# A speech codec kernel on one core: the silu's add of one on the pool engine, more updates on the vector engine, transposes and accumulating transfers taking turns

## The chip, the core and the metric

The kernel runs on one core of a Trainium2 chip. The metric is the device time of one execution in microseconds. The engines are named as the profile names them: PE is the tensor engine, DVE the vector engine, ACT the scalar engine, POOL the pool engine (GpSimd) and SP the engine that here only issues transfers. Each engine runs its own instructions in the order in which they were emitted.

## The reference

The input x is 2 x 16000 x 512 in bf16. The kernel must compute a depthwise convolution of three taps along time, a silu, four stages of residual vector quantization with eight code words each, and a second depthwise convolution of three taps over the sum of the chosen words:

```python
B, T, D, K = 2, 16000, 512, 3
Nq, C = 4, 8
z = sum(xp[:, i:i+T, :] * dw_enc[i] for i in range(K))
z = silu(z)
res, q = z, 0
for s in range(Nq):
    cb = codebooks[s]
    d2 = |res|^2 - 2 * res @ cb.T + |cb|^2
    sel = cb[d2.argmin(-1)]
    q, res = q + sel, res - sel
y = sum(qp[:, i:i+T, :] * dw_dec[i] for i in range(K))
```

## The kernel before

The 32000 tokens are cut into 250 groups of 128 tokens, and the groups into 16 chunks: one of 12 groups, 14 of 16, and one of 14 that is worked on as 16. The 512 channels are four channel blocks of 128. The encoder works with the channels on the partitions, so a tile of one channel block of a full chunk is 128 x 2048 bf16.

For each chunk:

- `load` brings x in transposed, by DMA transposes of four groups each that SP issues (line 486), into the tile XT. Chunk 0 is loaded as rows and turned on PE instead.
- `front` does the first convolution and the silu, one channel block at a time in `block(i)`. DVE multiplies by each of the three taps (line 553) into the tiles Z and T. The two sums Z + T are made either on DVE (line 561) or by an accumulating DMA that POOL issues (line 559); from chunk 1 on, the first sum of all four blocks and the second sum of block 3 are named in `DMA_ADDS`, five accumulating transfers a chunk. The silu is z / (1 + exp(-z)): ACT takes exp(-z) (line 565), an add of one follows on DVE (line 569), ACT takes the logarithm (line 573) and exp of its negative (line 576), and DVE multiplies with z into RES (line 581).
- `stage` runs four times. PE scores the tokens against the code words (lines 637 and 643), DVE reduces and picks the nearest word (lines 651 to 697), PE turns the one-hot choice (line 707) and DVE copies it (line 714). Then the residual is updated for each of four channel blocks, in two halves: either PE makes the chosen words alone and DVE adds them to RES (line 747, one operand from SBUF and one from PSUM), or PE adds RES and the words itself and ACT copies the result back (line 758). How many of the four blocks go by DVE in each of the first three stages is written in `ON_DVE`, and in `ON_DVE_LAST` for the last three chunks; the chunk's number picks the entry. The fourth stage has no update.
- `finish` makes the output by products of the one-hot choices with prepared tables (line 785), ACT copies them out of PSUM (line 791), and SP issues the stores (line 795).

The order of the work on each engine isn't written by hand. Every piece is a task of the class `Plan`, with an engine, a cost, a latency, what it needs, a due time and the buffers that it takes and gives. `Plan.run` simulates the tasks forwards and backwards from a seeded random start (`ROUNDS`) and emits the instructions in the order that comes out. All transfers are tasks of one server, "DMA". When the kind changes between transposes (RUNS, kind 1) and accumulating transfers (ADDS, kind 2), the plan adds a gap of up to `APART`, and it weighs such a gap by `CLUMP` when it picks the next transfer. What the hardware itself must wait for is set in `keep_apart`: each transpose waits for an accumulating transfer issued before it, and the other way round, and `LAG` says which one, counted back from the last.

Buffers: four of Z, five of T, three of E, one of LN, two of XT, three of YSB.

Of the kernel before, what the change touches and what calls it, by code (L numbers as in the profile page):

```python
# [13 lines left out]
ALU = mybir.AluOpType  # L14
# [11 lines left out]
SIZES = [12] + [16] * 14 + [14]  # L26


ON_DVE = [(1, 2, 2)]
ON_DVE_LAST = [(2, 2, 2)]  # L30
LAST = 3

# [3 lines left out]

EARLY = 1

RUN = 4

AHEAD = 40
# [2 lines left out]
PERIOD, LEAD, STAGE, LATE, SPREAD = 56, 0.4, 0.9, 0.3, 0.3  # L44
FAR = -3.3e38

ROUNDS = [(940, 0.3, 0.0, 7), (4101, 0.3, 2.0, 9), (5991, 0.3, 0.0, 7), (15520, 0.3, 0.0, 10)]


CELLS, COLUMNS, ROWS = range(3)  # L50
WHOLE = (CELLS, CELLS, 0, 0.0)
SWITCH, CLING, SLOW = 0.1, 10.0, 1.08
RUNS, ADDS = (1, 1, 0, 0.0), (2, 2, 0, 0.0)
APART, CLUMP = 0.5, 2.0

LAG = 2


class Plan:
# [18 lines left out]
    def pass_over(self, rank, backward=False):  # L78

        tasks = self.tasks  # L80
        needs = [t[3] for t in tasks]
        after = [[] for _ in tasks]
        for n, ds in enumerate(needs):
            for d in ds:
                after[d].append(n)
        if backward:
            needs, after = after, needs
        takes, gives = (7, 6) if backward else (6, 7)
        left = [len(d) for d in needs]
        engines = list(dict.fromkeys(t[0] for t in tasks))  # L90
        ready = {e: [] for e in engines}
        until = {e: 0.0 for e in engines}
        slots = dict(self.slots)
        for n, t in enumerate(tasks):
            if not left[n]:
                heapq.heappush(ready[t[0]], (rank[n], n))
        now, events, order, starts, before = 0.0, [], [], [0.0] * len(tasks), WHOLE
        sort, ended = 0, 0.0
        while True:
            going = True  # L100
            while going:
                going = False
                for e in engines:
                    if until[e] > now + 1e-9:
                        continue
                    passed, pick, least, gap = [], None, 0.0, 0.0
                    while e == "DMA" and ready[e]:
                        at, n = heapq.heappop(ready[e])
                        passed.append((at, n))
                        if all(slots[k] > 0 for k in tasks[n][takes]):  # L110
                            kind, lost = tasks[n][8][0], 0.0
                            if kind and sort and kind != sort:
                                lost = max(0.0, APART - (now - ended))
                            if pick is None or at + CLUMP * lost < least:
                                pick, least, gap = n, at + CLUMP * lost, lost
                    while e == "PE" and ready[e]:
                        at, n = heapq.heappop(ready[e])
                        passed.append((at, n))
                        if all(slots[k] > 0 for k in tasks[n][takes]):
                            here = tasks[n][8]  # L120
                            lost = self.between(here, before) if backward else self.between(before, here)
                            if pick is None or at + CLING * lost < least:
                                pick, least, gap = n, at + CLING * lost, lost
                    if pick is not None:
                        passed = [v for v in passed if v[1] != pick]
                        if e == "PE":
                            before = tasks[pick][8]
                        elif tasks[pick][8][0]:
                            sort, ended = tasks[pick][8][0], now + gap + tasks[pick][1]
                    while pick is None and ready[e]:  # L130
                        at, n = heapq.heappop(ready[e])
                        if all(slots[k] > 0 for k in tasks[n][takes]):
                            pick = n
                            break
                        passed.append((at, n))
                    for p in passed:
                        heapq.heappush(ready[e], p)
                    if pick is None:
                        continue
                    t = tasks[pick]  # L140
                    for k in t[takes]:
                        slots[k] -= 1
                    order.append(pick)
                    starts[pick] = now
                    until[e] = now + gap + t[1]
                    heapq.heappush(events, (now + gap + t[1], -1))
                    heapq.heappush(events, (now + gap + max(t[1], t[2]), pick))
                    going = True
            if len(order) == len(tasks):
                return starts, order  # L150
            now = events[0][0]
            while events and events[0][0] <= now + 1e-9:
                _, n = heapq.heappop(events)
                if n < 0:
                    continue
                for k in tasks[n][gives]:
                    slots[k] += 1
                for a in after[n]:
                    left[a] -= 1
                    if not left[a]:  # L160
                        heapq.heappush(ready[tasks[a][0]], (rank[a], a))
# [46 lines left out]
def kernel(  # L208
# [8 lines left out]
    nc = tc.nc  # L217
# [255 lines left out]
    def load(st, org):  # L473
        plan.part += 1
        g0, G, GP = st["g0"], st["G"], st["GP"]
        done = []
        if g0 == 0:
            load_rows(st, org)
            return

        def place():
            st["XT"] = xpool.tile([P, GC + 2, KT, P], BF16, name="XT")

        def run(n, m):
            g = g0 + n - 1
            t = nc.sync.dma_start_transpose(out=st["XT"][:, n:n + m, :, :].rearrange("p n i t -> p (n i) t"),
                                        in_=xv[:, g:g + m, :].rearrange("p g d -> p (g d)"))
            keep_apart(t, runs, adds)

        def edge(n):  # L490
            st["XE"] = const.tile([P, KT, P], BF16, name="XE")
            keep_apart(nc.sync.dma_start_transpose(out=st["XE"], in_=group_rows(0)), runs, adds)

        def shift(n):
            XT, XE = st["XT"], st["XE"]
            nc.gpsimd.tensor_copy(XT[:, n, :, 0:P - 1], XE[:, :, 1:P])
            for b in range(B):
                p = (b + 1) * HB - 1
                nc.gpsimd.memset(XT[:, n, :, p:p + 1], 0.0)
            if GP > G:  # L500
                nc.gpsimd.memset(XT[:, G + 2:GP + 2, :, :], 0.0)

        def behind():
            nc.gpsimd.tensor_copy(st["XT"][0:1, 0, 0, 0:2], XR[0:1, 1, 0:2])
            nc.gpsimd.tensor_copy(st["XT"][0:1, 0, 0, 2:4], CB4[0:1, 0:2])
            for b in range(B):
                p = b * HB + 32
                nc.gpsimd.tensor_copy(st["XT"][p:p + 1, 0, 0, 0:2], XR[p:p + 1, 0, 0:2])

        room = plan.add("SP", 0.0, 0.0, [], org - 2.2 * PERIOD, place, take=("XT",))  # L510
        if st["n"] == 1:
            room = plan.add("POOL", 0.8, 1.0, [room, book, chunks[0]["rows"]], early, behind)
            gate.append(room)
        inside = min(G + 2, S + 1 - g0)
        for n in range(0, G + 2, RUN):
            due = org - 2.2 * PERIOD + 0.01 * n
            m = min(RUN, inside - n)
            if m > 0:
                done.append(plan.add("DMA", 0.7 * m, 2.7 + 0.7 * m, [room], due, lambda n=n, m=m: run(n, m), mode=RUNS))
        if inside < G + 2:  # L520
            t = plan.add("DMA", 0.9, 3.2, [room], due, lambda: edge(G + 1), mode=RUNS)
            st["edge"] = plan.add("POOL", 1.0, 1.4, [t], due, lambda: shift(G + 1))
        st["loaded"] = done + [st.get("edge")]

    def front(st, org):
# [3 lines left out]
        def dve(full):  # L529
            return 0.1 + (full - 0.1) * f  # L530
# [14 lines left out]
        def block(i):  # L545
            plan.part += 1
            u = {}

            def product(k):
                name = "ZTU"[k]  # L550
# [15 lines left out]

            def one():
                e = u["E"][:, 0:G, :]
                nc.vector.tensor_scalar(out=e, in0=e, scalar1=1.0, scalar2=None, op0=ALU.add)  # L569

            def log():
                u["LN"] = lnpool.tile([P, GC, P], F32, name="LN")
# [25 lines left out]
            st["taps"].append(t)  # L598
            z = add_up(2, [z, t])
            e = plan.add("ACT", act(1.8), act(1.8) + 0.12, [z], due, exp, take=("E",))  # L600
            e = plan.add("DVE", dve(0.6), dve(0.6) + 0.1, [e], due, one)
            e = plan.add("ACT", act(1.8), act(1.8) + 0.12, [e], due, log, take=("LN",))
            e = plan.add("ACT", act(1.8), act(1.8) + 0.12, [e], due, inverse, give=("LN",))
            r = plan.add("DVE", dve(1.13), dve(1.13) + 0.1, [e] + [t for t in st["silu"][-1:]], due, silu,
# [285 lines left out]
```

## Time and profile before

| | before |
|---|---|
| median of the runs shown (3) | 744.69 us |
| lowest, highest | 741.8, 744.74 us |
| the profiled execution's own time | 742.04 us |
| its span | 740.3 us |
| mean granted clock of PE | 0.934 |

A profile is taken of one execution. Its span reaches from the first to the last instruction, and the execution's own time, measured as the others, lies 1.7 us above it. A line of the groups names the line of code, the engine, the operation, output and inputs with their shapes, and the count; then the busy time in us and the mean duration of one in ns; then how long the engine had been idle just before such instructions, and what ended that. A line of the stretches gives the busy time of every engine between two times. A line of the order of time begins with start and duration in us.

### The profile page before, as it was taken

The numbers are of one execution on the slowest core, as the hardware profiler recorded it, in microseconds if no ns is written. First come the engines' busy times: TensorE is split into PE (matmuls) and PEld (weight loads), VectorE is DVE, ScalarE is ACT, GpSimd is POOL, SyncE is SP. The second block draws the span as 40 slices with busy tenths as digits, with TensorE's granted clock in tenths as the row PEclk, the third lists the DMA queues.
The fourth block names the chain that finished last, engine by engine and source line by source line (L and its number), as shares of the span: only waits on it lengthen the run. The fifth ranks groups of instructions, "written<-read, shape, count | busy, mean of one in ns | idle before, by whom it ended". The sixth has DMA issues, their size and how long they took to land. (4 is left out here: it accounts for less than half of the span.)

```text
span 740.3 us, 23586 instructions
## 1 busy us (share of the span) xinstructions
PE 590.8 (80%) x10478; PEld 314.2 (42%) x10544; DVE 685.9 (93%) x1359; ACT 665.4 (90%) x539; POOL 81.7 (11%) x104
## 2 busy tenths in 40 slices
PE   5037687787987888986978888878988898989996
PEld 5023334344444444434444444444453444444543
DVE  6999989899999999997999999989999999998952
ACT  2688979899999999998899999989999999976576
POOL 3112101111101011100101111100111101100000
PEclk9566969999999999999799899999999999999999
DMA  7969795859696967839978875959896435320234
GB/s 178 189 130 182 135 200 104 141 122 201 182 174 158 209 133 164 165 116 143 188 171 177 175 165 143 182 132 174 172 210 136 131 64 152 87 88 2 88 143 199
DMA packets 160833, 111.14 MB, mean 150 GB/s; under 512 B 142426, under 2 KB 142811, under 8 KB 160603
## 3 DMA queue, kind: packets, MB, share of 16 engines
q1 hardware_dynamic: 148976, 69.61, 39.5%
q0 software_dynamic: 11472, 39.76, 29.9%
q8 instruction: 82, 1.34, 0.8%
q10 hardware_dynamic: 282, 0.26, 0.1%
q14 instruction: 21, 0.16, 0.1%
HBM read 2.39 MB, written 32.77 MB: 47 GB/s over the span
## 5 line engine op out<-in xcount | busy, mean ns | idle before, releaser
L758 ACT ACTIVATE RES<-NEW 128x1024 bf16<-128x1024 f32 (+1 forms) x218 | 218.5, 1043 | 28.6 <-PE NEW L731 21.9
L747 DVE TENSOR_TENSOR RES<-RES,SEL 128x1024 bf16<-128x1024 bf16 (+1 forms) x166 | 197.5, 1203 | 6.7 <-PE SEL L731 6.3
L643 PE MATMUL PS<-RES 128*64 128x80 bf16 (+1 forms) x8064 | 176.1, 203 | 11.2 <-DVE RES L581 9.7
L643 PEld LDWEIGHTS <-RES 128*64 128x64 bf16 x8064 | 172.8, 115 | 19.6 <-DVE RES L581 10.6
L752 PE MATMUL NEW<-RES,IDENT 128*128 128x512 bf16 (+1 forms) x436 | 137.7, 399 | 31.3 <-ACT RES L758 15.6
L791 ACT ACTIVATE YSB<-Y 128x1024 bf16<-128x1024 f32 (+1 forms) x126 | 126.6, 1061 | 8.4 <-PE Y L785 4.5
L565 ACT ACTIVATE E<-Z 128x2048 bf16<-128x2048 bf16 (+1 forms) x64 | 123.2, 1931 | 11.5 <-DMA Z<-T 4.0
L559 POOL DMA_DIRECT2D Z<-T x75 | 72.9, 976 | 537.5 <-ACT RES L758 78.8
L573 ACT ACTIVATE LN<-E 128x2048 f32<-128x2048 bf16 (+1 forms) x64 | 123.0, 1923 | 9.9 <-DVE E L569 9.2
L576 ACT ACTIVATE E<-LN 128x2048 bf16<-128x2048 f32 (+1 forms) x64 | 123.0, 1922 | 0.4
L651 DVE TENSOR_REDUCE TR<-PS 128x5 bf16<-128x320 f32 (+1 forms) x188 | 96.0, 515 | 14.4 <-PE PS L643 14.3
L553 DVE TENSOR_SCALAR T<-XT,WENC 128x2048 bf16<-128x2048 bf16 (+1 forms) x128 | 94.8, 745 | 5.1 <-DMA Z<-T 5.1
L731 PEld LDWEIGHTS <-CBN 32*128 32x128 bf16 x768 | 32.6, 92 | 137.7 <-issue 134.3
L785 PE MATMUL Y<-A,OHT 128*128 128x512 bf16 x219 | 77.6, 382 | 16.4 <-ACT RES L758 6.0
L731 PE MATMUL NEW<-OHT,CBN 32*128 32x512 bf16 (+1 forms) x436 | 88.3, 402 | 0.1
L581 DVE TENSOR_TENSOR RES<-Z,E 128x2048 bf16<-128x2048 bf16 (+1 forms) x64 | 77.3, 1208 | 0.0
L731 PE MATMUL SEL<-OHT,CBN 32*128 32x512 bf16 (+1 forms) x332 | 58.7, 396 | 22.0 <-ACT RES L758 13.3
L637 PE MATMUL PS<-MASK,IDENT 128*64 128x320 bf16 (+1 forms) x376 | 64.6, 340 | 8.6 <-DVE PR L654 6.2
L561 DVE TENSOR_TENSOR Z<-Z,T 128x2048 bf16<-128x2048 bf16 (+1 forms) x53 | 62.5, 1181 | 2.7 <-DMA Z<-T 2.7
L752 PEld LDWEIGHTS <-IDENT 128*128 128x128 bf16 x436 | 33.1, 99 | 67.4 <-issue 57.4
L430 PE MATMUL PS<-MASK,IDENT 128*128 128x384 bf16 x167 | 46.2, 359 | 10.1 <-DVE PR L654 9.8
L785 PEld LDWEIGHTS <-OHT 128*128 128x128 bf16 x373 | 32.1, 97 | 50.8 <-issue 22.8
(78 smaller groups left out, 416.2 us busy)
## 6 DMA issues: line engine op xcount, KB each, us to landing
Z<-T POOLq DMA_DIRECT2D x75, 512.0 KB, 5.6
out_dram<-YSB SPq DMA_DIRECT2D x61, 512.0 KB, 3.2
RES<-in_x_dram SPq DMA_DIRECT2D x1, 1664.0 KB, 6.8
XT<-in_x_dram SPq DMA_TRANSPOSE x74, 5.7
out_dram<-YSB SPq DMA_DIRECT2D x1, 384.0 KB, 2.3
out_dram<-YSB SPq DMA_DIRECT2D x1, 256.0 KB, 2.7
A<-in_dw_dec_dram POOLq DMA_DIRECT2D x2, 96.0 KB, 6.4
CB<-in_codebooks_dram ACTq DMA_DIRECT2D x1, 128.0 KB
```

What stands on the lines that cost most here:

```text
L553: nc.vector.tensor_scalar(out=places(u[name]), in0=taps(i, k), scalar1=WENC[:, i, k:k + 1], scalar2=None, op0=ALU.mult)
L565: nc.scalar.activation(u["E"][:, 0:G, :], u["Z"][:, 0:G, :], ACT.Exp, scale=-1.0)
L573: nc.scalar.activation(u["LN"][:, 0:G, :], u["E"][:, 0:G, :], ACT.Ln)
L576: nc.scalar.activation(u["E"][:, 0:G, :], u["LN"][:, 0:G, :], ACT.Exp, scale=-1.0)
L643: nc.tensor.matmul(V[h * HT:(h + 1) * HT, r, :], lhsT=half[:, LC:LC + HT], rhs=half[:, lo:hi], start=False, stop=(i == KT - 1), skip_group ...
L651: nc.vector.tensor_reduce(out=u["TR"][:, q:q + m], in_=u["V", q][:, :, own:own + HT], axis=AX.X, op=ALU.max)
L731: nc.tensor.matmul(ps, lhsT=CBN[s][rows, i * P:(i + 1) * P], rhs=u["OHT"][rows, 0:MB, :], start=start, stop=True, skip_group_check=True)
L747: nc.vector.tensor_tensor(out=old, in0=old, in1=u["SEL", i, j][:, :, 0:W].rearrange("p h (m t) -> p h m t", t=HT), op=ALU.add)
L752: nc.tensor.matmul(NEW[:, h, 0:W], lhsT=IDENT, rhs=tokens(i, j + h, 1), start=True, stop=False, skip_group_check=True)
L758: nc.scalar.activation(old, u["NEW", i, j][:, :, 0:W].rearrange("p h (m t) -> p h m t", t=HT), ACT.Copy)
L785: nc.tensor.matmul(Y[:, h, :], lhsT=lhs(), rhs=rhs, start=(a == 0), stop=(a == len(terms) - 1))
L791: nc.scalar.activation(u["YSB"][:, k:k + n, :], u[k][:, 0:n, :], ACT.Copy)
```

## The change

Four things are changed, and the seeds of the plan with them.

- From chunk 1 on, the add of one is issued on POOL in all four channel blocks, and the plan counts 2.4 us for it; in chunk 0 it stays on DVE.
- `ON_DVE` gets a second entry. Chunks 0, 2, ..., 12 take (2, 2, 2), chunks 1, 3, ..., 11 take (1, 2, 2) as before. The last three chunks are unchanged.
- `LAG` goes from 2 to 1: a transpose now waits for the last accumulating transfer issued before it rather than the last but one, and an accumulating transfer for the last transpose.
- In the plan, the gap after a change of kind becomes 1.9 us towards transposes and 2.3 us towards accumulating transfers, where it was 0.5 us, and the cost of a transpose falls from 0.7 to 0.6 us a group.

```diff
-ON_DVE = [(1, 2, 2)]
+ON_DVE = [(2, 2, 2), (1, 2, 2)]
 ON_DVE_LAST = [(2, 2, 2)]
...
+ONE_ON_POOL = (0, 1, 2, 3)
+POOL_ONE = 2.4
...
-ROUNDS = [(940, 0.3, 0.0, 7), (4101, 0.3, 2.0, 9), (5991, 0.3, 0.0, 7), (15520, 0.3, 0.0, 10)]
+ROUNDS = [(520, 0.3, 3.0, 9), (1278, 0.3, 0.0, 8), (1401, 0.3, 2.0, 6)]
...
-APART, CLUMP = 0.5, 2.0
-
-LAG = 2
+APART = (0.0, 1.9, 2.3)
+CLUMP = 2.0
+
+LAG = 1
...
-                                lost = max(0.0, APART - (now - ended))
+                                lost = max(0.0, APART[sort if backward else kind] - (now - ended))
...
-                done.append(plan.add("DMA", 0.7 * m, 2.7 + 0.7 * m, [room], due, lambda n=n, m=m: run(n, m), mode=RUNS))
+                done.append(plan.add("DMA", 0.6 * m, 2.4 + 0.6 * m, [room], due, lambda n=n, m=m: run(n, m), mode=RUNS))
...
+            on_pool = st["n"] >= EARLY and i in ONE_ON_POOL
...
             def one():
                 e = u["E"][:, 0:G, :]
-                nc.vector.tensor_scalar(out=e, in0=e, scalar1=1.0, scalar2=None, op0=ALU.add)
+                where = nc.gpsimd if on_pool else nc.vector
+                where.tensor_scalar(out=e, in0=e, scalar1=1.0, scalar2=None, op0=ALU.add)
...
-            e = plan.add("DVE", dve(0.6), dve(0.6) + 0.1, [e], due, one)
+            if on_pool:
+                e = plan.add("POOL", dve(POOL_ONE), dve(POOL_ONE) + 0.3, [e], due, one)
+            else:
+                e = plan.add("DVE", dve(0.6), dve(0.6) + 0.1, [e], due, one)
```

## The prediction

> **What bounds the kernel now.** I read four views in this order: the page's busy times, the busy time by stretches, the groups of instructions with shapes kept apart, and the list of what the vector engine waited for. Then I went to the order of time around the one place where the pool engine already does arithmetic on a whole tile. First the page's span and busy line, and the stretches. The columns of a stretch are its length, the busy time of PE, the weight loads, DVE, ACT and POOL with their counts, the granted clock, and the DMA share.
>
> ```profile
> span 740.3 us, 23586 instructions
> PE 590.8 (80%) x10478; PEld 314.2 (42%) x10544; DVE 685.9 (93%) x1359; ACT 665.4 (90%) x539; POOL 81.7 (11%) x104
> ```
>
> ```profile
> 60.00:160.00 100.00, 79.15 (x1340) 38.33 (x1341) 93.67 (x179) 91.24 (x70) 12.39 (x14) 0.85 0.80 147
> 160.00:260.00 100.00, 82.81 (x1557) 43.77 (x1561) 99.43 (x194) 98.80 (x82) 10.33 (x11) 1.00 0.86 181
> 260.00:360.00 100.00, 84.19 (x1479) 43.85 (x1488) 94.62 (x187) 94.89 (x78) 11.86 (x13) 0.93 0.76 149
> 360.00:460.00 100.00, 84.87 (x1576) 45.64 (x1585) 98.14 (x191) 97.48 (x81) 11.04 (x11) 0.97 0.78 172
> 460.00:560.00 100.00, 83.19 (x1483) 44.40 (x1494) 96.16 (x190) 96.70 (x79) 11.69 (x15) 0.97 0.87 170
> 560.00:640.00 80.00, 70.00 (x1307) 36.77 (x1318) 79.61 (x161) 78.34 (x65) 8.86 (x10) 0.98 0.45 114
> ```
>
> The reader is to see that between 60 and 640 us two engines are full at once. DVE sums to 561.6 us of 580, ACT to 557.5. TensorE has some 17% to spare and POOL nearly all. So work taken off DVE alone pays only until ACT is the longer, and anything that holds DVE up shows in the time nearly one to one. DVE has 18.4 us of idle time in that stretch; over the whole run its longest waits, the set-up left aside, are these (total, times, longest):
>
> ```profile
> DVE TR L651 <- PE PS L643: 14.3, 14, 3.4
> DVE RES L747 <- PE SEL L731: 6.3, 6, 2.0
> DVE T L553 <- DMA Z<-T: 5.1, 4, 4.2
> ```
>
> **The add of one leaves DVE.** The groups, each with its count, total, mean ns and idle time:
>
> ```profile
> L569 DVE TENSOR_SCALAR E<-E 128x2048 bf16<-128x2048 bf16 x60 | 41.6, 693 | 0.5 <-ACT E L565 0.5
> L747 DVE TENSOR_TENSOR RES<-RES,SEL 128x1024 bf16<-128x1024 bf16 x156 | 188.4, 1219 | 6.4 <-PE SEL L731 6.3
> L747 DVE TENSOR_TENSOR RES<-RES,SEL 128x768 bf16<-128x768 bf16 x10 | 9.1, 947 | 0.3 <-PE NEW L731 0.3
> L758 ACT ACTIVATE RES<-NEW 128x1024 bf16<-128x1024 f32 x204 | 207.6, 1060 | 27.4 <-PE NEW L731 20.8 <-PE SEL L731 6.5
> L758 ACT ACTIVATE RES<-NEW 128x768 bf16<-128x768 f32 x14 | 10.9, 804 | 1.1 <-PE NEW L731 1.1
> L553 DVE TENSOR_SCALAR T<-XT,WENC 128x2048 bf16<-128x2048 bf16 x120 | 90.0, 753 | 5.1 <-DMA Z<-T 5.1
> L553 DVE TENSOR_SCALAR Z<-XT,WENC 128x2048 bf16<-128x2048 bf16 x60 | 45.1, 752 | 0.0
> L581 DVE TENSOR_TENSOR RES<-Z,E 128x2048 bf16<-128x2048 bf16 x60 | 73.5, 1226 | 0.0
> L561 DVE TENSOR_TENSOR Z<-Z,T 128x2048 bf16<-128x2048 bf16 x45 | 55.0, 1222 | 2.7 <-DMA Z<-T 2.7
> L679 DVE TENSOR_TENSOR KEY<-V,GPOS 128x128 bf16<-128x128 bf16 x60 | 18.2, 304 | 0.2
> L684 DVE SCALAR_TENSOR_TENSOR KEY<-KEY,RANK 128x128 bf16<-128x128 bf16 x60 | 18.2, 303 | 0.2
> L673 DVE TENSOR_TENSOR V<-PR,TR 128x128 bf16<-128x128 bf16 x60 | 17.5, 291 | 0.2
> L697 DVE TENSOR_TENSOR OH<-KEY,M 128x128 bf16<-128x128 f32 x60 | 17.4, 290 | 0.1
> ```
>
> Chunks 1 to 15 have four channel blocks each, so all 60 full-size adds of line 569 move. Neighbours on DVE overlap by some 0.08 us (below: an instruction begun at 555.88 lasts 1.21, and the next begins at 557.01), so each frees 0.693 - 0.08 = 0.61 us, 37 us together.
>
> **The extra updates.** The seven even chunks 0, 2, ..., 12 use (2, 2, 2); the last three had that already. In stage 0 one channel block more, two instructions, goes by line 747 in place of line 758: 14 instructions, two of them in the short chunk 0. DVE gains 12 x (1.219 - 0.08) + 2 x (0.947 - 0.08) = 15 us; ACT loses 12 x 1.060 + 2 x 0.804 = 14 us. TensorE also loses the identity matmuls of those 14; it isn't the bound, so I price that at nothing. It costs nothing if the cover goes either, since it is work removed.
>
> **What the pool engine's add costs.** No add of this size runs on POOL in this trace. The nearest rows are one copy of 508 elements, the tiny copies, and, in order of time, what DVE did beside that copy (start, duration):
>
> ```profile
> L496 POOL COPY XT<-XE 128x508 bf16<-128x508 bf16 x1 | 0.6, 610 | 13.4 <-DMA XE<-in_x_dram 13.4
> L508 POOL COPY XT<-RES 1x2 bf16<-1x2 bf16 x2 | 0.4, 180 | 0.3 <-DMA RES<-in_x_dram 0.2
> ```
>
> ```profile
> 556.75 0.61 POOL L496 COPY XT<-XE 128x508 bf16<-128x508 bf16 x1 [13.38 <-DMA XE<-in_x_dram]
> ...
> 555.88 1.21 DVE L747 TENSOR_TENSOR RES<-RES,SEL 128x1024 bf16<-128x1024 bf16 x1
> 557.01 1.43 DVE L581 TENSOR_TENSOR RES<-Z,E 128x2048 bf16<-128x2048 bf16 x1
> ...
> L581 DVE TENSOR_TENSOR RES<-Z,E x64: 949/1219/1427, 28.0 to 658.3; 128x2048 bf16<-128x2048 bf16 x60, 128x1536 bf16<-128x1536 bf16 x4
> ```
>
> From 2 to 508 elements the copy grows by (610 - 180) / 506 = 0.85 ns each, so 2048 elements come to 0.18 + 2046 x 0.00085 = 1.92 us. That is an estimate, three times DVE's 0.69. The second reading matters more. The silu product of line 581 has minimum, median and maximum of 949, 1219 and 1427 ns. The maximum is the very one that began while the POOL copy was running: it was due at 557.09, the copy ended at 557.36, and it lasted 0.21 us longer than the median. The update of line 747, whose second operand lies in PSUM, ran beside the same copy at its usual 1.21. So a DVE instruction that takes all its operands from SBUF appears to wait until POOL has finished reading. It is one observation, but the only one of its kind, and it comes on the outlier.
>
> How much is that for 60 adds? The instructions of DVE that would be held are those with all operands in SBUF, lines 553, 561, 581 and the four small ones 673 to 697: 135.1 + 73.5 + 55.0 + 71.3 = 335 us. Of DVE's busy time after the change, 685.9 - 41.6 + 15 = 659, that is 51%. If POOL's 1.92 us falls anywhere, about 0.51 x 1.92 = 0.98 us of it holds DVE: 59 us for 60. The ends are 60 x 1.92 = 115 us (each add stops DVE for its whole length) and 0. A gain below nothing is excluded, since POOL takes nothing from DVE but the add already counted. I take 59, because the observed case was held for most of the 0.27 us in which the two met.
>
> The Trainium skill, page "SBUF — State Buffer", section "Who interferes with whom", says that DVE and GpSimd share a port pair by an exclusive lock. A DVE instruction in a two-port mode, or one with two SBUF inputs beside a GpSimd reader, and the GpSimd one block each other for the whole instruction. The row above agrees (+0.21 us). Read at its harshest it is the full-stop rival below.
>
> **The waits on POOL.** The add now stands in POOL's in-order queue and waits there for the exponential on ACT. Queued behind it are the issues of the accumulating transfers (line 559), whose results the next exponentials wait for. POOL's busy time grows from 82 to some 82 + 115 = 197 us of 740, so there is room. The four Z and five T buffers cover a few us, and I price this at nothing. With that cover gone ACT would wait for a late add; ACT has 14 us more slack then, and DVE is the later of the two.
>
> **Transposes and adds apart.** The rows of the queues and issues, and the wait of SP:
>
> ```profile
> q1 hardware_dynamic: 148976, 69.61, 39.5%
> q0 software_dynamic: 11472, 39.76, 29.9%
> ...
> Z<-T POOLq DMA_DIRECT2D x75, 512.0 KB, 5.6
> XT<-in_x_dram SPq DMA_TRANSPOSE x74, 5.7
> ```
>
> ```profile
> SPq L486 <- DMA Z<-T: 100.7, 18, 13.7
> ```
>
> With a lag of 1, a transpose waits for the last add issued before it, and an add for the last transpose. Queued behind a waiting transpose on SP are the output stores; behind a waiting add on POOL, now also the adds of one. The two queues use (39.5% + 29.9%) x 740.3 = 514 us of the engines' time. An accumulating transfer streams for 0.299 x 740.3 / 75 = 2.95 us and lands after 5.6, so each change of kind leaves about 2.65 us empty. The room is (740 - 514) / 2.65 = 85 changes, 5 to 6 a chunk. The plan's new gaps of 1.9 and 2.3 and its price on changing kind push it to clump, and XT is loaded two chunks ahead, so I price it at nothing within that room. By the Trainium skill, page "DMA: Bandwidth & Descriptors", section "Rules for kernel authors", a transpose next to ordinary transfers needs no separation, so nothing is bought either. No run here shows that yet.
>
> **The sum.** On DVE: -37 + 15 + 59 = +37 us. A DVE that runs late finds its inputs ready, so part of its 18.4 us of idle time goes: I take 8 of it back. Net +29 us. The profiled execution took 742.04 us (span 740.3) and the median of the shown runs is 744.69, 2.65 more; so 742 + 29 = 771 for a profiled one, and **774 us** as a median. The new search seeds in the plan change the order everywhere; I price that at nothing with 5 us either way.
>
> **Rivals.**
> *DVE isn't held (faster).* If the delays of line 581 don't scale, because POOL mostly runs beside updates and reductions that read PSUM, DVE gets 37 - 15 = 22 us shorter and ACT 14. With both full, the time falls by 14 to 22: 723 to 731. It turns at (37 - 15) / 60 = 0.37 us of hold per add; the row's 0.21 us for a copy a third as long speaks against it, and the 49% of DVE's time that reads PSUM or is not held speaks for it.
> *Near the turning point.* A hold of 0.3 to 0.4 us each ends at 741 to 748.
> *Full stop.* Each add stops DVE for all its 1.92 us: -37 + 15 + 115 - 8 = +85, so 830. Against it, nearly a third of DVE's time is line 747 alone, which ran undisturbed.
> *The transfers become the bound.* If the order alternates more than 85 times, say 100, the queues need 514 + 265 = 779 us, and the median is 782; DVE would then show waits for Z<-T and XT far above the 5.1 us quoted.
> *The change doesn't do what it says.* The lag binds only where kinds alternate in the order; where the plan has already clumped, it changes nothing. That is the case priced at nothing above.
>
> **How the numbers follow.** About 0.5% of the time, 3.7 us, is what a measurement of this kernel can tell from no change. Chances: the forecast 0.50, transfers as the bound 0.14, full stop 0.08, near the turning point 0.06, DVE not held 0.22. So faster 0.22, same 0.06, slower 0.72. The forecast's own range follows from holds of 0.65 to 1.35 us per add (-37 + 15 - 8 + 39 = +9, and +51): 754 to 796. The range over all cases, 724 to 806, leaves out the full stop, the lower end of the faster case and the upper end of the transfers: under 0.2 together.
>
> **What would show it.** Right: 60 POOL adds of about 1.9 us or more; lines 553, 561, 581 and 673 to 697 with longer means than the rows above, beside unchanged means of line 747 and 651; DVE at 93% or more of a longer span, ACT clearly below 90%. Line 569 left with four short adds; line 747 with 180 instructions, line 758 with 204. Wrong: those means unchanged and the span shorter; or DVE waiting for Z<-T or XT. The same total with unchanged means would refute my cause though not my number.

## The result and the profile after

The changed kernel takes 969.57 us (median of 4 runs, 960.41 to 974.63), the kernel before 743.25 us beside it. The ratio is 1.304, with a 95% interval of 1.293 to 1.315: 226 us slower. The forecast was 774 us, with a range from 724 to 806. The direction was right and the size far off.

The same lines of the page as before, span and busy times:

```profile
span 958.6 us, 23641 instructions
PE 667.9 (70%) x10550; PEld 344.7 (36%) x10550; DVE 891.6 (93%) x1313; ACT 664.3 (69%) x525; POOL 410.2 (43%) x164
```

DVE is as full as it was, of a span that is 218 us longer; ACT has fallen from 90% to 69%. So DVE is the only engine that is near full now, though 60 of its instructions were taken away. PE's granted clock is lower too, 0.812 against 0.934, and its busy time 77 us longer; but PE is busy for 70% of the span, and the rows below account for the time on DVE alone. The groups of the changed kernel (with shapes kept apart) show where its 206 us of additional busy time are:

```profile
L575 POOL TENSOR_SCALAR E<-E 128x2048 bf16<-128x2048 bf16 x60 | 334.8, 5580 | 247.2 <-ACT E L570 247.2
L756 DVE TENSOR_TENSOR RES<-RES,SEL 128x1024 bf16<-128x1024 bf16 x168 | 202.0, 1211 | 9.1 <-PE SEL L740 8.8
L558 DVE TENSOR_SCALAR T<-XT,WENC 128x2048 bf16<-128x2048 bf16 x120 | 175.8, 1469 | 0.1
L558 DVE TENSOR_SCALAR Z<-XT,WENC 128x2048 bf16<-128x2048 bf16 x60 | 103.0, 1718 | 0.0
L587 DVE TENSOR_TENSOR RES<-Z,E 128x2048 bf16<-128x2048 bf16 x60 | 95.4, 1590 | 3.5 <-PE PS L652 3.1 <-ACT E L582 0.4
L566 DVE TENSOR_TENSOR Z<-Z,T 128x2048 bf16<-128x2048 bf16 x45 | 64.1, 1423 | 0.0
L682 DVE TENSOR_TENSOR V<-PR,TR 128x128 bf16<-128x128 bf16 x60 | 38.4, 641 | 0.3
L693 DVE SCALAR_TENSOR_TENSOR KEY<-KEY,RANK 128x128 bf16<-128x128 bf16 x60 | 32.5, 543 | 0.1
L688 DVE TENSOR_TENSOR KEY<-V,GPOS 128x128 bf16<-128x128 bf16 x60 | 21.1, 353 | 0.2
L706 DVE TENSOR_TENSOR OH<-KEY,M 128x128 bf16<-128x128 f32 x60 | 20.5, 343 | 0.1
```

Against the rows of before, the tap products gained 85.8 + 57.9, the silu product 21.9, the sum 9.1 and the four small ones 20.9 + 14.3 + 2.9 + 3.1: 216 us, or 3.6 us for each of the 60 adds. (The extra updates add 15.7 us and the adds take 41.6 away, which would leave 190; neighbours on DVE overlap less than before, so its busy time grew by 206.) The update of line 756, with one operand in PSUM, stayed at 1211 ns. A mean of 1469 ns hides what happens. The order of time shows it, first around one add (POOL, then DVE):

```profile
396.51 5.82 POOL L575 TENSOR_SCALAR E<-E 128x2048 bf16<-128x2048 bf16 x1 [2.84 <-ACT E L570]
...
396.17 0.74 DVE L558 TENSOR_SCALAR T<-XT,WENC 128x2048 bf16<-128x2048 bf16 x1
396.83 0.28 DVE L706 TENSOR_TENSOR OH<-KEY,M 128x128 bf16<-128x128 f32 x1
397.03 5.85 DVE L558 TENSOR_SCALAR T<-XT,WENC 128x2048 bf16<-128x2048 bf16 x1
```

and then around another:

```profile
408.92 5.57 POOL L575 TENSOR_SCALAR E<-E 128x2048 bf16<-128x2048 bf16 x1 [5.75 <-ACT E L570]
...
408.53 0.74 DVE L558 TENSOR_SCALAR T<-XT,WENC 128x2048 bf16<-128x2048 bf16 x1
409.19 3.73 DVE L688 TENSOR_TENSOR KEY<-V,GPOS 128x128 bf16<-128x128 bf16 x1
412.83 1.21 DVE L756 TENSOR_TENSOR RES<-RES,SEL 128x1024 bf16<-128x1024 bf16 x1
```

A tap product of 0.74 us lasts 5.85, and a sum over 128 elements lasts 3.73 where its usual 0.30 would do. The profile counts this as busy time, so no list of waits shows it. The first ends 0.55 us after the add, which ended at 402.33. The second ends 1.57 us before its add, which ended at 414.49. The rest of the trace is alike: 57 of the 60 adds held a full-size DVE instruction by more than 0.15 us. The 38 tap products held end 0.54 or 0.55 us after their add. The 26 instructions held that have two SBUF operands end before it: by 1.56 to 1.59 us with 128 elements, by 0.64 or 0.65 with 2048.

ACT waits as well, for POOL's add, where it waited 9.2 us for DVE's before:

```profile
ACT LN L579 <- POOL E L575: 70.7, 32, 5.5
```

### The profile page after: what moved, and what is told of

Same layout as the page of the kernel before. It is cut to its first block, busy times and chain, and to the rows that moved or that the text cites. A ratio compares the mean times of both kernels' runs of the same rounds, so it can differ in the third digit from the quotient of the medians.

```text
span 958.6 us, 23641 instructions
## 1 busy us (share of the span) xinstructions
PE 667.9 (70%) x10550; PEld 344.7 (36%) x10550; DVE 891.6 (93%) x1313; ACT 664.3 (69%) x525; POOL 410.2 (43%) x164
## 4 chain that ended last, share of the span: by engine, by line
DVE 33%; PE 11%; issue 3%; ACT 2%; POOL 2%; DMA 0%; ACTq 0%; DVEq 0%; POOLq 0%
DVE RES L756 9%; DVE T L558 5%; DVE RES L587 4%; DVE Z L558 3%; DVE TR L660 3%; PE PS L652 3%; PE Y L794 3%; DVE Z L566 2%; DVE V L682 2%; DVE KEY L693 2%; POOL E L575 2%; PE NEW L761 2%; PE PS L646 1%; PE NEW L740 1%; DVE OH L706 1%
## 5 line engine op out<-in xcount | busy, mean ns | idle before, releaser
L575 POOL TENSOR_SCALAR E<-E 128x2048 bf16<-128x2048 bf16 x60 | 334.8, 5580 | 247.2 <-ACT E L570 247.2
L767 ACT ACTIVATE RES<-NEW 128x1024 bf16<-128x1024 f32 (+1 forms) x204 | 202.8, 1009 | 130.7 <-PE NEW L740 91.4
L756 DVE TENSOR_TENSOR RES<-RES,SEL 128x1024 bf16<-128x1024 bf16 (+1 forms) x180 | 213.2, 1194 | 9.2 <-PE SEL L740 9.0
L652 PE MATMUL PS<-RES 128*64 128x80 bf16 (+1 forms) x8064 | 201.2, 215 | 9.3 <-DVE RES L587 4.0
L652 PEld LDWEIGHTS <-RES 128*64 128x64 bf16 x8064 | 198.6, 126 | 19.3 <-DVE RES L587 4.5
L558 DVE TENSOR_SCALAR T<-XT,WENC 128x2048 bf16<-128x2048 bf16 (+1 forms) x128 | 180.6, 1415 | 0.1
L579 ACT ACTIVATE LN<-E 128x2048 f32<-128x2048 bf16 (+1 forms) x64 | 120.5, 1882 | 70.7 <-POOL E L575 70.7
L660 DVE TENSOR_REDUCE TR<-PS 128x5 bf16<-128x320 f32 (+1 forms) x188 | 94.8, 508 | 20.9 <-PE PS L652 20.7
L558 DVE TENSOR_SCALAR Z<-XT,WENC 128x2048 bf16<-128x2048 bf16 (+1 forms) x64 | 105.5, 1648 | 0.0
L740 PE MATMUL SEL<-OHT,CBN 32*128 32x512 bf16 (+1 forms) x360 | 70.7, 438 | 47.6 <-DVE RES L756 28.4
L587 DVE TENSOR_TENSOR RES<-Z,E 128x2048 bf16<-128x2048 bf16 (+1 forms) x64 | 99.2, 1551 | 3.5 <-PE PS L652 3.1
L794 PE MATMUL Y<-A,OHT 128*128 128x512 bf16 x249 | 90.5, 413 | 7.9 <-DVE OHT L723 2.2
L434 PE MATMUL PS<-MASK,IDENT 128*128 128x384 bf16 x201 | 66.0, 414 | 23.8 <-DVE PR L663 23.8
```

The lines of the kernel that those rows point to most:

```text
L558: nc.vector.tensor_scalar(out=places(u[name]), in0=taps(i, k), scalar1=WENC[:, i, k:k + 1], scalar2=None, op0=ALU.mult)
L575: where.tensor_scalar(out=e, in0=e, scalar1=1.0, scalar2=None, op0=ALU.add)
L579: nc.scalar.activation(u["LN"][:, 0:G, :], u["E"][:, 0:G, :], ACT.Ln)
L587: nc.vector.tensor_tensor(out=st["RES"][:, i, 0:2 * G, LC:LC + HT], in0=halves(u["Z"]), in1=halves(u["E"]), op=ALU.mult)
L652: nc.tensor.matmul(V[h * HT:(h + 1) * HT, r, :], lhsT=half[:, LC:LC + HT], rhs=half[:, lo:hi], start=False, stop=(i == KT - 1), skip_group ...
L660: nc.vector.tensor_reduce(out=u["TR"][:, q:q + m], in_=u["V", q][:, :, own:own + HT], axis=AX.X, op=ALU.max)
```

## The experiments

In all that keep an order of work, every engine runs its instructions in that order; only what the diff names is different. Ratios are to the kernel before, run beside them on the same chip.

**e1: the changed kernel, the add back on DVE.** Order and turns of the change are kept.

```diff
-                where = nc.gpsimd if on_pool else nc.vector
+                where = nc.vector
```

> The changed kernel with its order of work kept, only the 60 adds of one emitted on DVE again. Hold theory (a POOL add of 5.4 us keeps DVE instructions that take all operands from SBUF waiting, about 3.5 us each): the 208 us of waiting go, 60 x 0.61 = 37 us of adds come back, so 958.6 - 208 + 37 = about 790 as a profiled span, 750 to 800. Rival, the new order or the strict turns of transposes and accumulating transfers are the cause: the time stays above 900.

Measured: 769.41 us, ratio 1.032 (1.025 to 1.038). So 200 of the 226 us went with the engine of one instruction. DVE's busy time and the tap products fall back:

```profile
PE 602.6 (78%) x10487; PEld 321.8 (42%) x10550; DVE 703.2 (91%) x1373; ACT 657.1 (85%) x525; POOL 77.1 (10%) x104
L558 DVE TENSOR_SCALAR T<-XT,WENC 128x2048 bf16<-128x2048 bf16 x120 | 89.1, 746 | 3.9 <-DMA XT<-in_x_dram 2.4 <-DMA Z<-T 1.5
```

25 us remain that belong to the other parts of the change, with the adds on DVE in an order that was planned without them there.

**e2: the kernel before, only the add on POOL.** Its own order.

```diff
-                nc.vector.tensor_scalar(out=e, in0=e, scalar1=1.0, scalar2=None, op0=ALU.add)
+                where = nc.gpsimd if st["n"] >= EARLY else nc.vector
+                where.tensor_scalar(out=e, in0=e, scalar1=1.0, scalar2=None, op0=ALU.add)
```

> The kernel before with its order kept, only the 60 adds of chunks 1 to 15 emitted on POOL. Hold theory: 743 + 60 x (3.5 - 0.6) = 743 + 174 = 917, 890 to 950, with a mean add of 5.4 to 5.6 us and DVE at 93% or more. Rival, the order and the turns are the cause: under 800. Rival, the longer silu chain starves ACT: also slow, but with DVE below 85% busy.

Measured: 949.85 us, ratio 1.275 (1.264 to 1.286), at the upper end of the range expected. Both halves agree: the add costs 205 us on the old order and 200 on the new. The page's busy line and the add's group, whose mean is again far above 1.92 us:

```profile
PE 662.8 (70%) x10478; PEld 347.2 (37%) x10544; DVE 881.1 (93%) x1299; ACT 674.5 (71%) x539; POOL 410.0 (43%) x164
L570 POOL TENSOR_SCALAR E<-E 128x2048 bf16<-128x2048 bf16 x60 | 337.3, 5632 | 115.8 <-ACT E L565 115.7
```

DVE at 93% speaks against a silu chain that starves everything.

**e3: as e2, for channel block 3 alone.**

```diff
+                where = nc.gpsimd if st["n"] >= EARLY and i == 3 else nc.vector
```

> The kernel before with only the 15 adds of channel block 3 on POOL. Hold theory: each costs 3.5 - 0.6 = 2.9 us, 743 + 15 x 2.9 = 787, 770 to 800. If the harm comes from POOL's queue being crowded by 60 adds, a quarter of them does next to nothing: within 5 us of 743. If a few fit into the 18 us of idle time of DVE: 743 + 43 - 18 = 768.

Measured: 798.75 us, ratio 1.072 (1.065 to 1.080), 54 us for 15 adds: 3.6 us each, against 205 / 60 = 3.4 in e2. The price per add is much the same for 15 adds as for 60: DVE's idle time swallows none of it, and POOL was only 20% busy.

**e9: what POOL's instructions take alone.** Eight of them behind everything else, when DVE is idle. The sum at line 874 reads the same tile for both operands.

> The kernel before with eight POOL instructions behind everything else, where DVE is idle: the add of one on 2048, 1024 and 508 bf16 elements and on 1024 f32, copies of 2048 and 508, a fill of 2048, and a sum of two tiles. If an arithmetic instruction on POOL is slow by itself: the add of 2048 takes 5.3 to 5.4 us with nothing beside it, the copy of 508 0.61. If DVE slowed the adds in the changed kernel: about 1.9 us alone, as the prediction took from the copy.

The groups of POOL from 725 us on:

```profile
L866 POOL TENSOR_SCALAR RES<-RES 128x2048 bf16<-128x2048 bf16 x1 | 5.4, 5371 | 90.3 <-DVE RES L862 90.3
L874 POOL TENSOR_TENSOR RES<-RES 128x2048 bf16<-128x2048 bf16 x1 | 3.6, 3598 | 0.1
L866 POOL TENSOR_SCALAR RES<-RES 128x1024 bf16<-128x1024 bf16 x1 | 2.8, 2767 | 0.1
L866 POOL TENSOR_SCALAR RES<-RES 128x1024 f32<-128x1024 f32 x1 | 2.8, 2767 | 0.0
L872 POOL COPY RES<-RES 128x2048 bf16<-128x2048 bf16 x1 | 1.9, 1889 | 0.0
L873 POOL MEMSET RES<- 128x2048 bf16 x1 | 1.8, 1804 | 0.1
L866 POOL TENSOR_SCALAR RES<-RES 128x508 bf16<-128x508 bf16 x1 | 1.5, 1477 | 0.1
L872 POOL COPY RES<-RES 128x508 bf16<-128x508 bf16 x1 | 0.6, 610 | 0.1
```

The prediction's 1.92 us was right for a copy of 2048 (1.889) and wrong for the add, which takes 5.371 with nothing beside it. The shortest of the 60 adds of the changed kernel took 5.353. So DVE doesn't slow the adds much (mean 5.58); the adds stop DVE.

**e7: POOL only writes.** On the old order, three fills in place of each add; the sum of one is left out.

```diff
+                if st["n"] >= EARLY:
+                    for _ in range(3):
+                        nc.gpsimd.memset(e, 1.0)
+                    return
```

> As e2 (kernel before, its order), but each of the 60 adds on POOL is replaced by three fills of the same tile, which read nothing; the sum of one is left out. About the same POOL time (3 x 1.75 = 5.3 us). If it is POOL's reading that holds DVE's products and sums of two SBUF operands: lines for RES<-Z,E, Z<-Z,T and the four small ones at their old means (1.22, 1.22, 0.29 to 0.30 us), only the tap products (TENSOR_SCALAR) longer, and the time between 744 and 949, about 850. If POOL holds DVE whatever it does: all of them longer and about 950. If only the length of the silu chain matters: about 950 with means unchanged.

Measured: 863.13 us, ratio 1.159 (1.150 to 1.169). The groups of POOL's fills and of DVE:

```profile
L571 POOL MEMSET E<- 128x2048 bf16 x180 | 359.2, 1997 | 132.9 <-ACT E L565 125.8
L553 DVE TENSOR_SCALAR T<-XT,WENC 128x2048 bf16<-128x2048 bf16 x120 | 152.3, 1273 | 3.5 <-DMA Z<-T 3.5
L585 DVE TENSOR_TENSOR RES<-Z,E 128x2048 bf16<-128x2048 bf16 x60 | 73.0, 1216 | 15.5 <-ACT E L580 15.0 <-PE PS L647 0.6
L553 DVE TENSOR_SCALAR Z<-XT,WENC 128x2048 bf16<-128x2048 bf16 x60 | 69.2, 1153 | 0.0
L561 DVE TENSOR_TENSOR Z<-Z,T 128x2048 bf16<-128x2048 bf16 x45 | 54.6, 1214 | 0.8 <-DMA Z<-T 0.8
L683 DVE TENSOR_TENSOR KEY<-V,GPOS 128x128 bf16<-128x128 bf16 x60 | 17.8, 297 | 0.3
L677 DVE TENSOR_TENSOR V<-PR,TR 128x128 bf16<-128x128 bf16 x60 | 16.9, 281 | 0.3
L688 DVE SCALAR_TENSOR_TENSOR KEY<-KEY,RANK 128x128 bf16<-128x128 bf16 x60 | 17.8, 297 | 0.3
L701 DVE TENSOR_TENSOR OH<-KEY,M 128x128 bf16<-128x128 f32 x60 | 16.9, 282 | 0.2
```

All products and sums of two SBUF operands are at their old means although POOL is as busy as in e2; only the tap products wait. So a POOL instruction that only writes doesn't hold a DVE instruction with two SBUF operands, and it does hold the tap products. That it is the reading in POOL's add that holds the first kind is concluded from this one contrast, between a fill and an add. This run also shows a second cost. DVE's busy time is 62 us above the kernel before, but the time 117, and ACT waits for POOL:

```profile
ACT LN L577 <- POOL E L571: 100.5, 37, 7.5
```

So a chain that is some six microseconds longer (three fills of 2.0 us) doesn't look free, as the prediction had it. In the changed kernel ACT's 70.7 us of the same wait lie beside a DVE that is 93% busy; what they would cost there without DVE's stops no run shows.

**e4 and e8: no add at all.** The logarithm on ACT adds the one itself, which leaves out the rounding of the sum to bf16. e4 plans anew without the task; e8 keeps the task in the plan, and so the order, and emits nothing for it.

```diff
-                nc.scalar.activation(u["LN"][:, 0:G, :], u["E"][:, 0:G, :], ACT.Ln)
+                nc.scalar.activation(u["LN"][:, 0:G, :], u["E"][:, 0:G, :], ACT.Ln, bias=1.0)
```

> The kernel before without the add as an instruction: the logarithm on ACT takes its input plus a bias of one; the plan is made anew without that task. DVE loses 64 instructions, 37 + 2 us, ACT nothing. If DVE and ACT bound together: ACT's 665 us of work remain, so the time falls by less than 39, to 715 to 735. If the wait for DVE between the two ACT passes (9.2 us) was what counted: about 734.

> As e4 (the logarithm adds the one itself, which leaves out the rounding of the sum to bf16), but with the order of the kernel before kept: every engine's order is the same, only DVE's 64 adds are gone. If e4's 26 us of loss came from its new order: 710 to 735 here. If DVE's adds cost nothing because ACT and PE bind: 744 within 4 us.

Measured: e4 770.22 us, ratio 1.034 (1.028 to 1.041), and e8 737.21 us, ratio 0.991 (0.987 to 0.995). Both expected ranges were missed: e4 was to come to 715 to 735, and e8 lies between its two cases. The busy line of e8:

```profile
PE 590.9 (81%) x10544; PEld 313.4 (43%) x10544; DVE 655.0 (90%) x1295; ACT 665.3 (91%) x539; POOL 76.5 (10%) x104
```

DVE lost 31 us of busy time and the kernel about 8 us. With ACT at 91% and an order fixed beforehand, an add that costs nothing is worth 1%. And e4, with less work than the kernel before, is 26 us slower than it and 33 slower than e8, which has the same instructions on DVE, ACT and POOL: that is the order that came out of the new plan.

**e5, e6 and e11: the turns of transposes and accumulating transfers.** e5 is e1 with a lag of 2, e6 the kernel before with 1, e11 with 3; each on its own order.

```diff
-LAG = 2
+LAG = 1
```

> As e1 (the changed kernel's order, adds on DVE), but each transpose and accumulating transfer waits for the last but one of the other kind again; the order of every engine is that of e1. If the strict turns cost e1's 25 us over the kernel before: back to about 745. If the 25 us come from an order planned for another place of the add: 769 within 4 us.

> The kernel before with strict turns and nothing else; the order of every engine is kept. If the turns cost what e1 lost: 765 to 770. If they are hidden, as the prediction priced them: 744 within 4 us.

> The kernel before with looser turns (lag 3 in place of 2), order kept. e6 showed that turns cost 41 us on this order at lag 1. If lag 2 still costs something (the transposes on SP wait 100 us for Z<-T in the kernel before): 730 to 740. If lag 2 had hidden it all: 745 within 4 us.

Measured: e5 767.92 us, ratio 1.028 (1.021 to 1.035), the same as e1's 1.032; e6 786.33 us, ratio 1.056 (1.050 to 1.061); e11 743.04 us, ratio 1.001 (0.996 to 1.005). e6 is slower than both cases expected. Strict turns cost 41 us on an order that wasn't planned for them and nothing that can be measured on one that was. Among the waits for transfers in e6 are these; the last two took 7.9 and 100.7 us in the kernel before:

```profile
DVE Z L561 <- DMA Z<-T: 29.9, 15, 3.9
ACT E L565 <- DMA Z<-T: 12.9, 4, 6.8
POOL Z L559 <- DMA XT<-in_x_dram: 96.2, 8, 17.9
SPq L486 <- DMA Z<-T: 267.5, 28, 19.9
```

**e10: the changed kernel's order without any add**, by the same bias.

> The changed kernel's order with no add at all (the logarithm adds the one, which leaves out the rounding of the sum to bf16). This is the time the plan would have with an add that costs neither POOL nor DVE anything. If the 25 us of e1 come from 37 us of adds put where the plan had none: 730 to 745. If the new order is bad in itself: 755 or more.

Measured: 759.17 us, ratio 1.019 (1.011 to 1.026): the second case. This order would have been slower even with an add for nothing. Of e1's 25 us, 10 are the adds on DVE, and 14 to 16 the rest.

**e12: the kernel before with the change's search seeds.**

```diff
-ROUNDS = [(940, 0.3, 0.0, 7), (4101, 0.3, 2.0, 9), (5991, 0.3, 0.0, 7), (15520, 0.3, 0.0, 10)]
+ROUNDS = [(520, 0.3, 3.0, 9), (1278, 0.3, 0.0, 8), (1401, 0.3, 2.0, 6)]
```

> The kernel before with the changed kernel's line of search seeds and nothing else. e10 left 16 us that neither the add nor POOL explains. If they are the luck of the seeds (each line of seeds was found for its own set of costs): 755 to 775. If the extra updates, the gaps or the other costs in the plan are at fault: 743 within 6 us.

Measured: 775.55 us, ratio 1.048 (1.040 to 1.055), just above the range expected, with the same number of instructions on DVE, ACT and POOL in another order. An order found for other costs is 26 to 33 us worse (e4, e12), more than the rest that e10 leaves. So an order alone can cost as much as those 14 to 16 us; that it is their cause isn't shown. The extra updates were not tried by themselves, since they can't be changed without a new order. Nor was PE's granted clock: 0.899 to 0.912 in e10's runs, 0.922 to 0.935 in the fast runs of the kernel before beside them. The kernel before itself took 740.42 us at a clock of 0.935 and 751.07 at 0.914, so the lower clock goes with a longer time of that size; which of the two follows from the other is open. A plan made with the true 5.6 us for POOL's add, in place of 2.4, wasn't tried either.

## Why the prediction failed

It came out slower by the mechanism that was forecast, and not by luck: the signs listed under "What would show it" are all there, from the longer means of the held lines to the unchanged 1211 ns of the update. The sizes failed. By its steps:

- *What bounds the kernel*: DVE and ACT together. This held before the change. e8 shows that the adds alone, off DVE for nothing, are worth about 8 us on the old order. The gain of 14 to 22 us in the rival "DVE isn't held" was more than that, but it also took 14 us off ACT, which e8 doesn't.
- *The add leaves DVE (-37), the extra updates (+15 on DVE, -14 on ACT)*: line 756 gained 213.2 - 197.5 = 15.7 us, line 767 lost 218.5 - 202.8 = 15.7.
- *What the pool engine's add costs*: this step failed. It took the price of an arithmetic instruction from a copy, 1.92 us; the add takes 5.37 alone and 5.58 in place. The copy row gave no bound from above for another operation, so the 115 us called the upper end was none: DVE's held instructions grew by 216 us where 59 were forecast.
- *The share that holds DVE*: 51% predicted, 3.6 / 5.58 = 64% measured. With 5.58 us and the predicted share, 60 adds would come to 171 us; with the measured share, to 216. So most of the miss is the cost and the rest the share. A share of DVE's time was also the wrong form: DVE works in order, so once it comes to an instruction that POOL holds, it stands until that is released, as the 5.85 and 3.73 us above show. The single delayed product at 557.01, on which the step rested, was read rightly, though one row was thin ground.
- *The lock by the Trainium skill*, page "SBUF — State Buffer", section "Who interferes with whom": the traces agree on who holds whom, the write-only case of e7 among it (1216 and 1214 ns unchanged). The page says "for the whole instruction" of the two-port modes; the prediction said it of both kinds. It holds for the tap products, which end 0.55 us behind the add, but not for instructions with two SBUF operands: the sum of line 688 ended 1.57 us before its add did.
- *The waits on POOL, priced at nothing*: ACT waits 70.7 us for POOL in the changed kernel, and 100.5 in e7. In the changed kernel 210 us of loss from the adds go beside 216 us on DVE, so these waits added nothing that can be told; in e7 the time grew by 55 us more than DVE's busy time.
- *Transposes and adds apart, priced at nothing*: right for the changed order (e5 beside e1), wrong as a rule (e6, 41 us). Nothing was bought by it: e5 and e1 are equal.
- *The 8 us taken back from DVE's idle time*: not seen. Span less busy time on DVE went from 54 us to 67.
- *The seeds, 5 us either way*: too narrow. The same seeds cost 33 us on the old costs (e12); what they cost in the changed kernel was not measured by itself.

The sum comes out with measured terms. From e10 to the changed kernel the order is the same, and the adds on POOL come in, with the four short ones of chunk 0 on DVE: 969.57 - 759.17 = 210 us, beside 216 us by which DVE's instructions grew. The other 14 to 16 us are what e10 lies above the kernel before, with the cause open as said. The 37 us credited for freeing DVE never appeared in full: from e1 to e10, the same adds taken off DVE gave 10 us, and from before to e8 about 8.

None of these runs that does the whole computation is faster than the kernel before; a lag of 3 equals it.

## What to carry to other kernels

Before work is moved from the vector to the pool engine, measure the very instruction there, alone; another operation of the same shape is no price (1.9 against 5.4 us). Then count, for each such instruction, how long the vector engine goes on before it meets an instruction with all operands in SBUF. Most of what is left of the pool engine's time was lost here (3.6 of 5.6 us an add), and shows as longer instructions and not as waits. Where an order is searched for given costs, compare parts of a change on one fixed order: a new one alone moved this kernel by 3 to 5%.

## What the runs showed of the hardware

- On POOL over 2048 bf16 elements a fill took 1.80 us, a copy 1.89, a sum of two operands, here the same tile twice, 3.60, and an add of a constant 5.37. The add of a constant is the slowest of the four, and took the same 2767 ns for 1024 elements in bf16 and f32.
- A DVE instruction with two SBUF operands was released about 1.9 us before the end of POOL's add (408.92 + 5.57 = 414.49, against 412.92 - 0.30 = 412.62; with 2048 elements, 0.65 + 1.22 gives the same), a tap product only at its end. Two of the three adds that held nothing show the same limit: DVE came to a product or sum of two SBUF operands 3.77 us after the start of an add of 5.58, and 3.89 after the start of one of 5.71, and each took its usual 1.21 or 1.22 us. 3.7 us and 1.9 us are close to POOL's 3.60 for a sum and 1.80 for a fill. That the add reads first and writes at the end is a guess from these numbers.
- Strict turns alone shortened a transpose, from issue to landing, from a median of 5.7 us to 4.8 in e6, which was 41 us slower all the same. In the changed kernel it took 4.6.
